# Attention and a top-1 mixture of experts on one core: the ninth block of k and q in the tile of x's transposes, and a batch's finish step by step at named places

## The chip, the core and the metric

The kernel runs on one core of a Trainium2 chip: TensorE (PE in the rows) multiplies matrices, VectorE (DVE), ScalarE (ACT) and GpSimd (POOL) work on tiles, and the queues of SyncE (SP) and GpSimd start transfers. Each engine has its own instruction stream and runs it in order; semaphores join the streams. The metric is device time in microseconds, from one execution of the whole program. Matmul results lie in PSUM; here three buffers of two banks each (`ps_s`) serve nearly all of attention.

## What is computed

Block-causal attention over 8 batches of 8 heads, 576 positions and 64 dimensions each, then a mixture of experts in which each of the 4608 rows goes to the one expert with the largest gate logit:

```python
scores = np.where(mask, scale * np.matmul(q, k.transpose(0, 1, 3, 2)), -1000000000.0)
attn = np.exp(scores - np.max(scores, axis=-1, keepdims=True))
attn = attn / (np.sum(attn, axis=-1, keepdims=True) + 1e-09)
x = np.matmul(attn, v)                      # then [B * S, H * D]

logits = x @ w_gate
e_idx = np.argmax(logits, axis=1)
probs = softmax(logits)                     # sum + 1e-9
eom = 1.0 / (1.0 + np.exp(-(x @ w_output_gate)))
for e in range(E):
    mask = e_idx == e
    h = np.maximum(x[mask] @ w1[e], 0.0)
    out[mask] = gate_w[mask, None] * eom[mask, e, None] * (h @ w2[e])
```

## The kernel before, in words

**Pairs, periods, rounds.** Attention goes over 32 pairs (8 batches by 4 pairs of heads). A pair passes through the stages fetch, turn, maxima, probabilities, values, norm, transposes of x; the pairs overlap like a pipeline. `round_of(g)` writes one round, four rounds (`r` = g mod 4) are one **period**, in which each stage handles one pair. Four periods are one **cycle**, a batch. I number periods by q = g // 4, so q mod 4 is the place in the cycle (period 0, 1, 2, 3). TensorE, ScalarE and VectorE run in the order in which the Python code is written (`manual_schedule`); GpSimd and the queues are ordered by a scheduler that follows the code.

**The period.** It begins with max_odd (L193 on TensorE, its maximum L340 on VectorE) and max_tile 0 (L186); then prob_tile 3 of the pair before (L240), norm (L293 to L297), prob_tiles 0 and 1 (L212), max_tiles 1 and 2 (L177 on VectorE) and max_rest (L198); then values_odd and values (L264 to L266). In the fourth round `turn` transposes eight of the nine 128-row blocks of a later pair's k and q into one `ps_s` tile (L123); ScalarE copies them to float16 (L127) and VectorE subtracts to get the low part (L128). `turn_max` transposes the maxima (L326) into bank 0 of another tile, puts the **ninth block** (r = 0) into bank 1 of the same tile, and converts it on VectorE (a small L127 and a small L128). `spare[0]` keeps that tile: max_odd of the next period writes its scores into both of its banks, columns 320 to 384. `turn_x` transposes a finished pair's x (L311) in a third tile, from which ScalarE copies (L313, L314). On GpSimd a period has `lpcr` and five `lpc` (L255, low parts of the probabilities, read from SBUF) and one `vl` (L151), which values need (L265). In the last four pairs the `lows` of L255 are VectorE's.

**The finish of a batch.** When a batch's x is transposed, `turn_x` hangs the generator `finish_batch` into the list `later`. Each call of `pay_later` runs one step of it, up to the next `yield`. There are eight calls in a period, three of them in the third round. The steps: gate logits `lgT` on TensorE (L494) and their copy; transposes (L502) and the sum `L` (L504); `mx` and `eq` (L510, L513); `eq` times `erev` and `er` (L515, L517); `oh` and `d` (L519 to L525); the exponential of `d` and the gate's `z` and `zs` (L527 to L531); the matmuls of the ranks (L535 to L540) and the running count (L544, L545); `rk` and `rank` (L548, L550); `sl` and `sli` (L554, L556); `se` (L560, L561); `zs` and the reciprocal (L563, L564); then five **scatters** into the slot table (`tab_d`, L567), one per step. It begins one round after the last transposes of x, which are in period 2, so nearly all of it lies in period 3.

**The seam.** The last finish runs while the first steps of the experts are being built (`ahead`), one step of each in turn. `route_rest` counts rows per expert and builds the table of steps (L584 to L720); GpSimd fetches slots (`ids`, L743) and gathers rows (`xg`, L754), which ScalarE and VectorE turn into `xr` (L866, L867) in front of `h` (L905) and `y` (L934). After that TensorE works on experts to the end.

## Time and profile before

| | |
|---|---|
| three runs, median (lowest to highest) | 817.33 us (815.25 to 818.15) |
| the profiled execution, its own time | 811.65 us |
| its span, first to last instruction | 810.0 us, granted clock 0.972 |
| busy, share of the span | PE 697.3 us (86%), DVE 558.4 (69%), ACT 444.2 (55%), POOL 405.9 (50%) |
| attention's steady cycles | from 50.78 to 320.82 us, periods 4 to 27 |
| seam between attention and experts | some 400 to 455 us |

The average of busy time hides two stages. In the second half TensorE is busy nearly throughout; in the first none of the engines is. So the rows below are taken by stage: the periods of one cycle, the waits in attention, one ordinary period and one with a finish in order of time, and a few rows of the seam. A period is cut where L340 starts on VectorE. The granted clock is 1.00 when TensorE was granted 2.4 GHz throughout a stretch; a lower share means that part of it was granted 1.2 GHz.

### The profile page before, as it was taken

What the parts mean: (1) busy time and instruction counts of PE and PEld (TensorE: products, weight loads), DVE (VectorE), ACT (ScalarE), POOL (GpSimd) and SP (SyncE); (2) the same over time, 40 slices, a digit from 0 to 9 for tenths busy, and PEclk for the clock granted to TensorE, in tenths of its full rate; (3) what the DMA queues carried; (4) which work ended last, traced back from release to release, by engine and by line L of the source; (5) the groups of instructions that cost most, each with busy time, mean ns of one, the idle gap of its engine ahead of it and who ended that gap; (6) DMA issues with size and microseconds to landing.
All of it is one profiled execution on the core that took longest, in us unless ns stands there. A gap on an engine that the chain in (4) does not pass through costs nothing. (4 is left out here: it accounts for less than half of the span.)

```text
span 810.0 us, 24437 instructions
## 1 busy us (share of the span) xinstructions
PE 697.3 (86%) x9931; PEld 517.4 (64%) x9950; DVE 558.4 (69%) x1000; ACT 444.2 (55%) x606; POOL 405.9 (50%) x404
## 2 busy tenths in 40 slices
PE   4889787879878787776796899999999999999994
PEld 3577665757667575655664566856667566686652
DVE  7577777877777877879362877956688666795530
ACT  2556454655546564545321867855587655885530
POOL 3777596987869696636725732222332343210001
PEclk9999999999999999998999999999999999999998
DMA  6555436263534635253108799789999979931601
GB/s 153 134 123 129 101 84 150 56 155 81 133 94 97 148 67 136 61 175 120 32 2 285 159 284 288 247 272 300 326 297 358 317 159 324 231 73 42 233 28 42
DMA packets 207850, 131.61 MB, mean 162 GB/s; under 512 B 161552, under 2 KB 180016, under 8 KB 207728
## 3 DMA queue, kind: packets, MB, share of 16 engines
q1 hardware_dynamic: 199680, 110.66, 49.6%
q0 software_dynamic: 8048, 19.29, 7.9%
q8 instruction: 80, 1.31, 0.8%
q14 instruction: 42, 0.34, 0.2%
HBM read 127.08 MB, written 19.34 MB: 181 GB/s over the span
## 5 line engine op out<-in xcount | busy, mean ns | idle before, releaser
L905 PEld LDWEIGHTS <-w1b 128*128 128x128 f16 (+1 forms) x2208 | 176.1, 98 | 25.1 <-DVE w1b L784 3.6
L905 PE MATMUL ps_s<-xt,w1b 128*128 128x256 f16 (+5 forms) x1920 | 175.8, 253 | 2.7 <-DVE w1b L784 2.2
L934 PE MATMUL ps_o<-w2b,hh 128*128 128x512 f16 (+1 forms) x541 | 164.9, 384 | 4.5 <-ACT hh L913 4.5
L784 DVE TENSOR_TENSOR w2b<-w2f,w2b 128x1024 bf16<-128x1024 f32 x80 | 92.6, 1219 | 88.8 <-ACT w2b L782 88.8
L255 POOL TENSOR_TENSOR lpc<-pc 128x512 f16<-128x512 f32 x140 | 140.9, 1041 | 7.6 <-ACT pc L248 7.2
L943 POOL DMA_INDIRECT out_dram<-ys,ids x38 | 49.4, 1300 | 163.0 <-ACT ys L942 89.3
L934 PE MATMUL ps_o<-w2b,hl 128*128 128x512 f16 x280 | 107.3, 383 | 1.4 <-DVE hl L914 0.5
L934 PEld LDWEIGHTS <-hh 128*128 128x128 f16 x560 | 54.9, 99 | 67.4 <-ACT hh L913 4.7
L784 DVE TENSOR_TENSOR w1b<-w1f,w1b 128x1024 bf16<-128x1024 f32 x80 | 92.9, 1216 | 3.2 <-ACT w1b L782 3.0
L177 DVE TENSOR_REDUCE nmz<-ps_s 128x2 bf16<-128x896 f32 (+3 forms) x128 | 82.7, 692 | 15.5 <-PE ps_s L193 14.9
L942 ACT ACTIVATE ys<-ps_o,ids 128x512 f32<-128x512 f32 (+1 forms) x38 | 26.1, 686 | 116.9 <-PE ps_o L934 101.5
L248 ACT ACTIVATE pc<-ps_s 128x1024 f32<-128x1024 f32 (+1 forms) x96 | 78.2, 882 | 19.5 <-PE ps_s L212 18.8
L782 ACT CAST w1b<-w1f 128x1024 f16<-128x1024 f32 x80 | 78.4, 1045 | 4.9 <-DMA w1f<-in_moe_w_dram 4.9
L128 DVE TENSOR_TENSOR tr<-ps_s,tr 128x1024 f16<-128x1024 f32 (+1 forms) x62 | 47.9, 772 | 44.2 <-ACT tr L127 43.2
L782 ACT CAST w2b<-w2f 128x1024 f16<-128x1024 f32 x80 | 77.6, 1043 | 0.1
L754 POOL DMA_INDIRECT xg<-x_d,ids x38 | 49.4, 1301 | 38.9 <-DVE xr L867 12.3
L264 PE MATMUL ps_v<-vh,pc 128*128 128x65 f16 x640 | 68.1, 198 | 0.0
L265 PE MATMUL ps_v<-vl,pc 128*128 128x64 f16 x640 | 67.7, 196 | 0.0
L266 PE MATMUL ps_v<-vh,lpc 128*128 128x65 f16 x640 | 67.4, 196 | 0.0
L255 POOL TENSOR_TENSOR lpcr<-pcr 128x640 f16<-128x640 f32 x28 | 35.2, 1257 | 62.6 <-ACT pcr L248 62.6
L264 PEld LDWEIGHTS <-pc 128*128 128x128 bf16 x640 | 60.0, 100 | 7.2 <-issue 7.1
L265 PEld LDWEIGHTS <-pc 128*128 128x128 bf16 x640 | 60.4, 101 | 0.6
(216 smaller groups left out, 1467.7 us busy)
## 6 DMA issues: line engine op xcount, KB each, us to landing
w1f<-in_moe_w_dram SPq DMA_DIRECT2D x80, 512.0 KB
w2f<-in_moe_w_dram SPq DMA_DIRECT2D x80, 512.0 KB
nat<-in_k_dram SPq DMA_DIRECT2D x64, 128.0 KB
nat<-in_q_dram SPq DMA_DIRECT2D x64, 128.0 KB
vn<-in_v_dram SPq DMA_DIRECT2D x64, 128.0 KB
x_d<-xn SPq DMA_DIRECT2D x32, 256.0 KB
vn<-in_v_dram SPq DMA_DIRECT2D x64, 32.0 KB
hh<-in_moe_w_dram SPq DMA_DIRECT2D x4, 512.0 KB
```

The source lines that it names most:

```text
L177: last_max[0] = nc.vector.tensor_reduce(o, ps[:, :, c0:c1], AX.X, ALU.max, negate=True)
L248: last_exp[0] = nc.scalar.activation(self.pt[i], ap, AF.Exp, scale=SCALE)
L255: eng.tensor_tensor(self.pl[i][:, sl], self.pt[i][:, sl], self.high(i)[:, sl], ALU.subtract)
L264: nc.tensor.matmul(o, hi, self.vh[rows, j], start=first, stop=False)
L265: nc.tensor.matmul(o[:, 0:D], hi, self.vl[rows, j], start=False, stop=False)
L266: nc.tensor.matmul(o, lo, self.vh[rows, j], start=False, stop=last)
L754: nc.gpsimd.indirect_dma_start(out=xg[i % NXG][0:width[i], h], out_offset=None, in_=x_d[0:nx, :], in_offset=IOA(ap=ids[i][0:width[i], h, 0 ...
L782: nc.scalar.copy(hi, src)
L784: eng.tensor_tensor(lo[at], src[at], hi[at], ALU.subtract)
L905: nc.tensor.matmul(ph[:, f4].rearrange("p (h n) -> p h n", n=w), wv[:, cc, f, :], xv[:, cc], start=(k == 0), stop=(k == 3 * KD - 1))
L934: nc.tensor.matmul(py, hv[:, f, h], wv[:, f, :], start=(k == 0), stop=(k == 3 * KF - 1))
L943: nc.gpsimd.indirect_dma_start(out=out, out_offset=IOA(ap=ids[i][0:w, h, 0:1].bitcast(U32), axis=0), in_=ys[0:w], in_offset=None, bounds_c ...
```

## The change

The ninth block goes from `turn_max`'s tile into that of x's transposes: `turn_rest` takes a tile, runs `turn_x`'s five transposes into it, transposes the ninth block into columns 128 to 256 of its bank 1, then lets ScalarE copy x, then converts the block on VectorE. `max_odd` still takes `turn_max`'s tile, in which only the maxima now lie. Every `yield` of `finish_batch` names a kind of place, and `pay_later(kind)` runs a step only at a place of the kind that it waits for: "m" and "n" behind max_rest, "v" behind the first values, "y" at the end of the fourth round. The running count moves ahead of the rank matmuls, the exponential of `d` behind them. Two scatters go to a step instead of one. In the loop behind the last round, `pay_later()` without a kind runs every step.

```diff
-        def turn_x(self):
+        def turn_x(self, pa):
...
-            pa = banks().rearrange("p a n -> p (a n)")
             for t in range(NT):
                 nc.tensor.transpose(pa[:, P * t:P * t + P], self.xn[:, t], ident)
+            yield
             xT = xTs[self.b]
...
     def turn_max(p):
-        z, y = pairs[p], pairs[p + 2] if p + 2 < NPR else None
+        z = pairs[p]
...
-        if y:
-            y.turn_blocks(ps[:, 1:2, 0:P], 0)
         z.qe = sb.tile([P, 640], BF16, name="qe")
         nc.scalar.copy(z.qe, pm[:, 0:640])
+
+    def turn_rest(p, p9):
+
+        ps = banks()
+        flat = ps.rearrange("p a n -> p (a n)")
+        x = pairs[p].turn_x(flat) if 0 <= p < NPR else iter(())
+        y = pairs[p9] if p9 < NPR else None
+        next(x, None)
         if y:
-            y.halves(ps[:, 1:2, 0:P], 0, nc.vector.tensor_copy)
+            y.turn_blocks(ps[:, 1:2, P:2 * P], 0)
+        next(x, None)
+        if y:
+            y.halves(ps[:, 1:2, P:2 * P], 0, nc.vector.tensor_copy)
...
-    def pay_later():
+    want = {}
+
+    def pay_later(kind=None):
         for g in list(later):
-            if next(g, later) is later:
-                later.remove(g)
+            if kind is None or want.get(g) in (None, kind):
+                want[g] = next(g, later)
+                if want[g] is later:
+                    later.remove(g)
...
     def finish_batch(b, xT):
-        yield
+        yield "v"
         lgT = sb.tile([P, S], F32, name="lgT", bufs=1)
...
         nc.scalar.copy(lgT, pm[:, 0:S])
-        yield
+        yield "y"
...
-        yield
+        yield "m"
         lg, lz = L[:, :, 0:E], L[:, :, E:2 * E]
...
         nc.vector.tensor_tensor(eq, lg, mxb, ALU.is_equal)
-        yield
...
         nc.vector.tensor_reduce(er, eq, AX.X, ALU.max)
-        yield
+        yield "n"
...
-        yield
-        nc.scalar.activation(d, d, AF.Exp)
+        yield "v"
...
-        yield
+        add = small.tile([P, E], F32, name="add")
+        nc.vector.tensor_reduce(add, oh.rearrange("p t e -> p e t"), AX.X, ALU.add)
+        nc.vector.tensor_tensor(run_cnt[:, b + 1], run_cnt[:, b], add, ALU.add)
+        yield "y"
+        nc.scalar.activation(d, d, AF.Exp)
         nc.scalar.activation(zs, zs, AF.Exp, scale=-1.0)
...
-        yield
+        yield "m"
         sl = small.tile([P, NT], F32, name="sl")
...
-        yield
+        yield "n"
         nc.vector.scalar_tensor_tensor(zs, zs, 1.0, se, ALU.add, ALU.mult)
...
             scatters.append(sc)
-            yield
+            if t % 2 == 0:
+                yield
...
         elif r == 2:
...
-            pay_later()
-            pay_later()
+            pay_later("m")
+            pay_later("n")
             do(10, "values", 0)
-            pay_later()
+            pay_later("v")
             do(6, "lows", 2)
         else:
             do(-5, "turn")
             if g < 4 * NPR:
                 turn_max(g // 4)
-            do(15, "turn_x")
-            pay_later()
+            if g < 4 * NPR + 8:
+                turn_rest(g // 4 - 3, g // 4 + 2)
+            pay_later("x")
             do(11, "values", 1)
         for fn in events.get(g, ()):
             fn()
-        pay_later()
+        pay_later("abwy"[r])
```

What this does to the streams, at three places. First TensorE at the end of an ordinary period, before (L326 the last transpose of the maxima, L123 the ninth block, L311 x's, L264 the values):

```order
L326 LDWEIGHTS nmz_97
L326 MATMUL ps_s<-identb,nmz_97 128x128
L123 MATMUL ps_s<-ident,nat 128x128
L311 MATMUL ps_s<-ident,xn 128x128 x5
L264 LDWEIGHTS pc_2136
```

and after (L327 and L310 are the old L326 and L311):

```order
L327 LDWEIGHTS nmz_97
L327 MATMUL ps_s<-identb,nmz_97 128x128
L310 MATMUL ps_s<-ident,xn 128x128 x5
L123 MATMUL ps_s<-ident,nat 128x128
L264 LDWEIGHTS pc_2103
```

The ninth block changed places with x's transposes, and tiles with them.

Second, VectorE. Before, in period 3, from the last maxima (L198) to the big conversion and what follows:

```order
L198 TENSOR_REDUCE nmz_97<-nm_2957 128x2
L515 TENSOR_TENSOR eq<-eq,erev 128x40
L517 TENSOR_REDUCE er<-eq 128x5
L519 MEMSET er 64x1
L521 TENSOR_TENSOR oh<-er,erev 128x40
L525 TENSOR_TENSOR d<-L,mx 128x40
L529 TENSOR_TENSOR z<-L,oh 128x40
L531 TENSOR_REDUCE zs<-z 128x5
L544 TENSOR_REDUCE add<-oh 128x8
L545 TENSOR_TENSOR run_cnt<-run_cnt,add 128x8
L128 TENSOR_TENSOR tr_3198<-ps_s,tr_3197 128x1024
L127 CAST tr_3197<-ps_s 128x128
```

After, the same batch one period later, in period 0 (L524 to L546 are the old L510 to L545):

```order
L198 TENSOR_REDUCE nmz_96<-nm_3237 128x2
L524 TENSOR_REDUCE mx<-L 128x5
L527 TENSOR_TENSOR eq<-L,mx 128x40
L528 TENSOR_TENSOR eq<-eq,erev 128x40
L530 TENSOR_REDUCE er<-eq 128x5
L532 MEMSET er 64x1
L534 TENSOR_TENSOR oh<-er,erev 128x40
L538 TENSOR_TENSOR d<-L,mx 128x40
L541 TENSOR_TENSOR z<-L,oh 128x40
L543 TENSOR_REDUCE zs<-z 128x5
L545 TENSOR_REDUCE add<-oh 128x8
L546 TENSOR_TENSOR run_cnt<-run_cnt,add 128x8
```

The block stands whole between the last maxima and the big conversion (L128 is the next row), where `mx` and `eq` stood earlier before. `sl` to the reciprocal stand at the same place of period 1, `L` (L518) ahead of the first maximum of period 0.

Third, GpSimd around the scatters. Before, in period 0:

```order
L255 TENSOR_TENSOR lpc_2141<-pc_2137 128x512
L567 DMA tab_d<-idg,sli 37120x2 x3
L151 TENSOR_TENSOR vl_104<-vn_99,vh_102 128x640
L567 DMA tab_d<-idg,sli 37120x2 x2
L255 TENSOR_TENSOR lpcr<-pcr 128x640
```

After, in period 1:

```order
L255 TENSOR_TENSOR lpc_2408<-pc_2404 128x512
L151 TENSOR_TENSOR vl_103<-vn_100,vh_101 128x640
L576 DMA tab_d<-idg,sli 37120x2 x5
L255 TENSOR_TENSOR lpcr<-pcr 128x640
```

All five scatters now stand behind `vl`, one period later.

## Rows read from the trace of the kernel before

**Rows 1.** Busy time by windows: the four periods of one cycle (12 to 15).

```profile
139.95:149.41 9.46, 8.55 (x205) 7.00 (x203) 8.22 (x19) 5.96 (x9) 7.29 (x7) 1.00 0.38 92
149.41:159.23 9.82, 8.54 (x205) 7.05 (x203) 7.18 (x15) 5.96 (x9) 8.88 (x9) 1.00 0.15 29
159.23:169.81 10.58, 9.65 (x221) 7.46 (x219) 7.18 (x15) 6.07 (x10) 10.58 (x11) 1.00 0.55 129
169.81:184.41 14.60, 9.63 (x216) 7.90 (x214) 11.18 (x32) 6.93 (x12) 8.75 (x8) 1.00 0.70 169
```

Columns: stretch and length in us; busy us (and instructions) of PE, PE's weight loads, DVE, ACT, POOL; granted clock; DMA share; GB/s.

**Rows 2.** The same view, whole cycles: the first, the fourth, the last.

```profile
50.78:95.19 44.41, 37.11 (x829) 30.39 (x827) 32.72 (x77) 24.96 (x39) 30.70 (x29) 0.96 0.52 123
184.41:231.93 47.52, 39.14 (x829) 31.31 (x827) 33.81 (x81) 24.93 (x39) 35.53 (x33) 0.93 0.46 107
276.38:320.82 44.44, 36.36 (x829) 29.40 (x827) 33.77 (x81) 24.93 (x39) 35.49 (x33) 1.00 0.46 106
```

**Rows 3.** TensorE's waits, 20 to 390 us: total, times, longest.

```profile
PE ps_s L535 <- DVE oh L521: 22.6, 7, 5.7
PE ps_s L193 <- DVE tr L128: 17.6, 16, 2.2
PE ps_s L311 <- DVE tr L128: 11.1, 6, 2.0
PE ps_v L265 <- POOL vl L151: 2.5, 9, 0.4
```

**Rows 4.** VectorE in time, period 13: start, length, instruction, idle before it.

```profile
155.48 0.17 DVE L198 TENSOR_REDUCE nmz<-nm 128x2 bf16<-128x4 f32 x1
157.18 1.23 DVE L128 TENSOR_TENSOR tr<-ps_s,tr 128x1024 f16<-128x1024 f32 x1 [1.54 <-ACT tr L127]
...
158.64 0.29 DVE L128 TENSOR_TENSOR tr<-ps_s,tr 128x128 f16<-128x128 f32 x1
```

**Rows 5.** TensorE in time, the end of period 13.

```profile
158.99 0.20 PE L193 MATMUL ps_s<-tr 64*128 64x64 f16 x2 [1.03 <-DVE tr L128]
```

**Rows 6.** VectorE in time, a finish (period 15), and one row of the seam.

```profile
174.98 0.19 DVE L510 TENSOR_REDUCE mx<-L 128x5 f32<-128x40 f32 x1
175.20 0.70 DVE L513 TENSOR_TENSOR eq<-L,mx 128x40 f32<-128x40 f32 x1
...
177.15 0.75 DVE L515 TENSOR_TENSOR eq<-eq,erev 128x40 f32<-128x40 f32 x1
...
178.93 0.20 DVE L529 TENSOR_TENSOR z<-L,oh 128x40 f32<-128x40 f32 x1
...
179.53 0.17 DVE L545 TENSOR_TENSOR run_cnt<-run_cnt,add 128x8 f16<-128x8 f16 x1
...
183.38 0.17 DVE L554 SCALAR_TENSOR_TENSOR sl<-er,rank 128x5 f32<-128x5 f32 x1
...
188.67 0.89 DVE L563 SCALAR_TENSOR_TENSOR zs<-zs,se 128x5 f32<-128x5 f32 x1
...
406.48 0.19 DVE L515 TENSOR_TENSOR eq<-eq,erev 128x40 f32<-128x40 f32 x1
```

**Rows 7.** GpSimd in time, from a scatter's period to the next finish.

```profile
141.75 1.25 POOL L255 TENSOR_TENSOR lpcr<-pcr 128x640 f16<-128x640 f32 x1 [4.82 <-ACT pcr L248]
143.05 5.04 POOL L255 TENSOR_TENSOR lpc<-pc 128x512 f16<-128x512 f32 x5
...
161.91 1.39 POOL L151 TENSOR_TENSOR vl<-vn,vh 128x640 f16<-128x640 f32 x1
...
173.81 5.03 POOL L255 TENSOR_TENSOR lpc<-pc 128x512 f16<-128x512 f32 x5 [0.75 <-ACT pc L248]
```

**Rows 8.** The seam in time: VectorE, GpSimd, TensorE.

```profile
431.31 0.43 DVE L715 TENSOR_REDUCE rt<-pc 128x35 f32<-128x280 f32 x1
440.36 1.08 POOL L754 DMA_INDIRECT xg<-x_d,ids  x1 [2.82 <-DMA ids<-tab_d]
446.81 0.43 PE L934 MATMUL ps_o<-w2b,hh 128*128 128x512 f16 x1 [4.54 <-ACT hh L913]
```

More of the change, by code (lines that the diff above doesn't have):

```diff
@@ L542, in finish_batch @@
         )
-        add = small.tile([P, E], F32, name="add")
-        nc.vector.tensor_reduce(add, oh.rearrange("p t e -> p e t"), AX.X, ALU.add)
-        nc.vector.tensor_tensor(run_cnt[:, b + 1], run_cnt[:, b], add, ALU.add)
-        yield
         rk = small.tile([P, NT, E], F32, name="rk")
@@ L561, in finish_batch @@
         nc.vector.tensor_scalar(se, se, 1e-9, None, ALU.add)
-        yield
+        yield "n"
         nc.vector.scalar_tensor_tensor(zs, zs, 1.0, se, ALU.add, ALU.mult)
@@ L576, in finish_batch @@
             scatters.append(sc)
-            yield
+            if t % 2 == 0:
+                yield
     def counts(col, name):
@@ L1040, in round_of @@
             if g == 4 * NPR + 9:
-                do(13, "turn_x")
+                turn_rest(NPR - 1, NPR)
         elif r == 2:
```

## The prediction, made before the changed kernel ran

> **What bounds the kernel now.** I read the busy time by windows first, since attention and experts have different limits. The four periods of one cycle of attention (one batch) last 9.46, 9.82, 10.58 and 14.60 us, 44.46 in all, and no engine fills them: TensorE is busy 36.37 us, GpSimd 35.50, VectorE 33.76 [rows 1]. The fourth period, in which almost all of a batch's finish lies, has hardly more TensorE work than the third (9.63 against 9.65) and takes 4.02 us longer: there VectorE and the waits rule. Such a cycle repeats: the first and the last of the six whole ones last 44.41 and 44.44 us, and one is 47.52 us at a granted clock of 0.93 [rows 2], so the level of 1.2 GHz was granted in a part of it. Then I asked who waits for whom on TensorE in attention [rows 3]. Two waits lead: the rank matmuls (L535) for `oh`, 22.6 us in 7, and the maxima of a new period (L193) for VectorE's L128, 17.6 us in 16; then the transposes of x (L311) for the same L128, 11.1 in 6. The change aims at all three. The wait for `vl` from GpSimd (L265) is small today, 2.5 us in 9, but it says that GpSimd is just in time.
>
> Behind about 455 us the experts begin in earnest; what is gained before that point moves their start and, as long as their weights have been loaded, the end.
>
> **The ninth block.** Today it sits in bank 1 of the tile that the next max_odd writes. In the period from 149.41 VectorE converts the eight blocks at 157.18 for 1.23 us and the ninth at 158.64 to 158.93 [rows 4]; TensorE's L193 starts at 158.99 after 1.03 us of waiting for that [rows 5]. After the change L193 needs only ScalarE's copy of the turned maxima, and max_tile 0 behind it needs the eight-block conversion, which ended at 158.41: 0.5 us earlier. What is late next is max_rest's prob_tile 3, which takes the buffer of x's transposes and so waits for the ninth block's conversion and two copies; it stands some 0.4 us behind. So I give back 0.15 to 0.2: **0.35 us per period**, bounds 0 (prob_tile 3 comes exactly as late as now) and 0.6. The ninth block turns after x's transposes instead of before; that is one matmul of the same kind at another place, so nothing. This alone is some 1.4 us a cycle, and a quiet period becomes 9.46 − 0.35 = 9.1.
>
> **The finish, period by period** (S is a period's start, cover is the time that VectorE has free). Free time lies between the last maxima and the big conversion: L198 ends at 155.65, L128 starts at 157.18, 1.5 us [rows 4].
>
> Period 3 of the cycle (the old place): it loses all but the gate logits and their sum. The logits cost TensorE 1.1 us (9.65 against 8.54 busy in rows 1) and move here, ahead of the turn; their copy goes ahead of ScalarE's conversion, 0.25 us more, and the sum L over 320 columns stands behind the small conversion and ahead of the next maxima, 0.7 with its own wait. 9.1 + 1.1 + 0.25 + 0.7 = 11.2, before GpSimd is asked.
>
> Period 0 takes `mx` to `run_cnt`. These eleven operations took 0.9 us from 174.98 to the end of `eq`, and 2.55 from 177.15 to the end of `run_cnt` at 179.70 [rows 6]: 3.4 us in 1.5 of cover, so the big conversion, and with it max_tile 0, comes 1.9 to 2.0 us later. The rank matmuls then follow, no longer waiting for `oh`, and `rk` and `rank` stand ahead of the next maxima: 0.6. 9.1 + 2.0 + 0.6 = 11.7.
>
> Period 1 takes `sl` to the reciprocal: `zs` 0.89, `sl` 0.17 and four like `run_cnt`'s 0.17 and `z`'s 0.20 [rows 6], with their gaps 2.15 us in 1.5 of cover: 9.1 + 0.7 = 9.8. Period 2 has lost the logits: 9.1.
>
> One thing can make these dearer. `eq` and L515 took 0.70 and 0.75 us while GpSimd worked on `lpc` (173.81 to 178.84 in rows 7); L515 took 0.19 at 406.48, and `z` took 0.20 at 178.93, just behind that work [rows 6]. In the new places `d`, `z`, `run_cnt` and `sl` can meet GpSimd's `lpc` or `vl`, 0.5 us each: 0 to 1.5 us in period 0, 0 to 0.5 in period 1. In period 0 `lpc` ended 8.1 us behind S (148.09 against 139.95), and in the new order `vl`, 1.39 us long, follows it at once, where `oh`, `d` and `z` stand. I take half of the upper end, 0.7: period 0 becomes 12.4. In period 1 I take 0, since what follows hides it. The Trainium skill says of this (SBUF — State Buffer, Who interferes with whom) that a VectorE instruction with both inputs in SBUF contends with a GpSimd instruction that reads SBUF. The 0.75 against 0.19 us agree, and by that rule whatever of the finish falls beside `vl` costs its upper end, 44.3 us a cycle instead of the 43.5 below.
>
> **GpSimd.** Its five scatters move one period on, and all of them behind `vl`. From the `lpcr` at 141.75 to the end of the `vl` two periods on at 163.30 they and two periods' `lpcr`, `lpc` and `vl` (7.7 us each) fill 21.55 us, so a scatter costs 1.2 and there is hardly a pause [rows 7]. That `vl` ended 4.1 us behind the start of its period (159.23) and TensorE waited at most 0.4 for one [rows 3], so I put the need at 3.9. With the scatters in period 1, where `lpcr` can start 2.25 us behind S (1.8 in the row, and the later prob_tile 3 ahead of it), that chain ends at 23.8; the values of period 3 need it at 9.8 + 9.1 + 3.9 = 22.8. TensorE waits 1.0 us: period 3 becomes 12.2. The sum is 12.4 + 9.8 + 9.1 + 12.2 = **43.5 us against 44.46**. The wait also caps it: whatever is saved in periods 1 and 2 is only waited for in 3.
>
> **The whole.** Six whole cycles lie between 50.78 and 320.82, 270.0 us. At 43.5 they would be 261.0, −9.0, of which 3 us is the one disturbed cycle; I keep half of that, for a stretch of the lower clock that can come again elsewhere, and take −7.5. The first four periods have only the ninth block: −1. The last four pairs add VectorE's own `lows` work and are bound by VectorE, which keeps its operations: −1.5 (0 to −3). At the seam to the experts [rows 8] the last finish is paid in fewer, larger steps: by its order the reciprocal and the scatters come about 1 us earlier, and the table of steps (`rt` at 431.31) no longer stands behind the second tile of x. GpSimd's second gather at 440.36 and with it `xr` and `w1b` come some 4 us earlier, and TensorE, which sat 4.54 us before 446.81, starts step 1 without that hole. Against it, ScalarE now makes four `xr` before the two `hh`. I take −3.5 of a possible 4.5, and 0 as the other bound. Together −7.5 − 1 − 1.5 − 3.5 = −13.5 from the profiled execution's 811.65. That execution is 5.7 us below the median of 817.33 and 3.6 below the fastest of the three runs; I carry the difference over to the median: 803.8, **804 us**.
>
> **Rivals.** (a) *GpSimd becomes the bound.* The scatters now all stand between `vl` and the next `lpcr`. If they start 2 us later than I think, because the reciprocal comes late, the wait for `vl` in period 3 is 3 us instead of 1 and a cycle is 45.5; six are then 273, 3 longer than now. With the seam, the end of attention and the start this is −3: 814. For it speaks that GpSimd is in time by a few tenths today; against it that GpSimd is busy only 35.50 of 44.46 us.
> (b) *Slower: VectorE's block of finish ahead of the conversion idles TensorE long enough to lose the clock.* In period 0, 3.4 to 4.9 us stand in a row ahead of the conversion that max_tile 0 needs. TensorE then idles 2 to 3.4 us at one place in every cycle. In the cycle of 47.52 us the clock was 0.93 and 3 us were lost [rows 2]. If each cycle loses half of that and a little more, 1.7 us, and the rest of the dear ends, 1.3, comes on top, a cycle is 46.5: six are 279, 9 longer than now. Less the seam's 3.5 and 1 at the start: +4.5, 822. It decides from the point at which TensorE's pause in period 0 exceeds those that pass without a lower clock today; in the fourth period of rows 1 TensorE waits for `oh` and the clock stayed at 1.00, which speaks against it.
> (c) *The finish vanishes altogether.* If the waits on VectorE are absorbed by the three buffers, a cycle goes to 9.1 four times, plus 2.05 for the logits with their copy and sum, plus half of what I add in periods 0 and 1, 40; GpSimd's floor is 35.5 and TensorE's 36.4. Six cycles then give −30, less the half stretch of lower clock −28, with the rest −34: 783.
> (d) *The change doesn't do what it says*: max_tile 0 and prob_tile 3 come as late as max_odd does now, and the finish only changes its period. Then a cycle stays at 44.5, and only the seam's gain is left, partly: 815.
>
> **How the numbers follow.** A measurement of this kernel can tell about 0.3%, 2.4 us, from no change; the three runs before lie 2.9 us apart. Chances: the forecast 0.56 (795 to 812: the rest of the dear ends and no gain at the end of attention on one side, the cheap end of period 0, the seam's 4.5 and an undisturbed clock on the other), (a) 0.16, (b) 0.12, (c) 0.09, (d) 0.07. Faster: 0.56 + 0.09 of (a), which lies on the edge, + 0.09 = 0.74; within 0.3%: 0.07 of (a) + 0.07 = 0.14; slower: 0.12. To hold 8 in 10 the range takes in the forecast, (a), (d), the mild part of (b), and a little of the way to (c): 790 to 819.
>
> **What would show it.** Right: L193's wait for L128 is gone from TensorE's list, and so is L535's for `oh`; periods of a cycle near 12.4, 9.8, 9.1, 12.2; L265's wait for `vl` grown to about 1 us per batch, only in period 3; the second gather near 436. Wrong: a granted clock below 0.97 with a drop in each period 0 points to (b); waits for `vl` of 3 us to (a); a cycle near 40 to (c); L186 or L240 waiting for L128 as long as L193 did to (d). The term that I trust least is period 0, where one row of operations decides between 11.7 and 13.2 us.

## The result and the profile after

The changed kernel takes 819.65 us (median of 20), the kernel before 812.38 (20): ratio 1.008, interval 1.0056 to 1.0103. It is slower by 0.8%, and just outside the forecast of 804 us (790 to 819). The forecast took 13.5 us off a median of 817.33, that of three runs; the twenty put the kernel before at 812.38, from which the same 13.5 would lead to 799. The profiled execution has a span of 817.7 us against 810.0 and a mean granted clock of 0.947 against 0.972.

One whole cycle in windows, in the columns of [rows 1] (periods 12 to 15 again):

```profile
135.84:147.96 12.12, 8.60 (x199) 7.21 (x200) 11.32 (x29) 6.41 (x11) 7.65 (x7) 0.97 0.53 125
147.96:160.54 12.58, 9.95 (x207) 7.84 (x206) 10.67 (x22) 5.96 (x9) 8.65 (x8) 0.90 0.41 98
160.54:172.27 11.73, 10.24 (x202) 8.10 (x199) 7.11 (x16) 6.07 (x9) 10.75 (x11) 0.85 0.48 85
172.27:183.66 11.39, 10.36 (x220) 8.13 (x221) 7.59 (x17) 6.51 (x10) 8.40 (x8) 1.00 0.51 120
```

The cycle takes 47.8 us where it took 44.46. Period 3 is 3.2 us shorter; period 0 is 2.7, period 1 2.8 and period 2 1.15 us longer. The clock of 0.90 and 0.85 gives a part of the reason for periods 1 and 2: TensorE was granted 1.2 GHz for a part of the time. TensorE's waits from 20 to 390 us, beside [rows 3] (L551 is the old L535; L186 is max_tile 0):

```profile
PE ps_s L551 <- DVE tr L128: 19.3, 6, 3.2
PE ps_s L186 <- DVE tr L128: 17.1, 17, 2.6
...
PE ps_v L265 <- POOL vl L151: 3.6, 1, 3.6
```

The waits that the change aimed at (L193 and L311 for L128, L535 for `oh`) are gone. Two others stand in their place: the rank matmuls, and max_tile 0 (L186), behind period 1 above all, now wait for the *big* conversion. The one wait for `vl` is in period 31. In time:

```profile
147.24 0.19 PE L551 MATMUL ps_s<-oh,below 128*128 128x40 f16 x1 [3.22 <-DVE tr L128]
...
160.15 0.34 PE L186 MATMUL ps_s<-tr 64*128 64x384 f16 x2 [2.58 <-DVE tr L128]
```

And in windows of one microsecond behind the first of them:

```profile
149.00:150.00 1.00, 1.00 (x32) 0.71 (x26) 0.96 (x4) 0.16 (x1) 0.00 (x0) 0.50 0.38 85
150.00:151.00 1.00, 1.00 (x18) 0.61 (x16) 0.97 (x4) 0.55 (x1) 0.38 (x1) 0.72 0.86 195
```

A granted clock of 0.50 is 1.2 GHz: behind the wait TensorE works without a gap, at half speed. Why the big conversion is late, on VectorE:

```profile
143.95 1.44 DVE L538 TENSOR_TENSOR d<-L,mx 128x40 f32<-128x40 f32 x1
...
155.04 0.38 DVE L565 SCALAR_TENSOR_TENSOR sl<-er,rank 128x5 f32<-128x5 f32 x1
155.46 0.97 DVE L567 TENSOR_SCALAR sli<-sl 128x5 int32<-128x5 f32 x1
...
156.56 0.87 DVE L570 TENSOR_SCALAR se<-se 128x5 f32<-128x5 f32 x1
157.53 1.25 DVE L572 SCALAR_TENSOR_TENSOR zs<-zs,se 128x5 f32<-128x5 f32 x1
...
158.92 1.18 DVE L128 TENSOR_TENSOR tr<-ps_s,tr 128x1024 f16<-128x1024 f32 x1
```

and GpSimd in the same time:

```profile
143.93 1.40 POOL L151 TENSOR_TENSOR vl<-vn,vh 128x640 f16<-128x640 f32 x1
...
152.36 5.04 POOL L255 TENSOR_TENSOR lpc<-pc 128x512 f16<-128x512 f32 x5 [0.48 <-ACT pc L248]
157.35 1.41 POOL L151 TENSOR_TENSOR vl<-vn,vh 128x640 f16<-128x640 f32 x1
```

Beside `lpc` or `vl`, `sl` took 0.38 us, `sli`, the addition to `se` and `zs`, all of five columns, 0.87 to 1.25, and `d`, forty columns, 1.44. From `sl` to the reciprocal's end at 159.0 it is 3.95 us.

### The profile page after: what moved, and what is told of

The parts are those of the page before. It is cut to its first block, busy times and chain, and to the rows that moved or that the text cites. A ratio compares the mean times of both kernels' runs of the same rounds, so it can differ in the third digit from the quotient of the medians.

```text
span 817.7 us, 24522 instructions
## 1 busy us (share of the span) xinstructions
PE 710.9 (87%) x9931; PEld 525.0 (64%) x9950; DVE 576.2 (70%) x1000; ACT 443.9 (54%) x606; POOL 402.1 (49%) x404
## 5 line engine op out<-in xcount | busy, mean ns | idle before, releaser
L255 POOL TENSOR_TENSOR lpc<-pc 128x512 f16<-128x512 f32 x140 | 140.9, 1040 | 5.9 <-ACT pc L248 5.1
L953 POOL DMA_INDIRECT out_dram<-ys,ids x38 | 47.2, 1242 | 160.0 <-ACT ys L952 81.2
L952 ACT ACTIVATE ys<-ps_o,ids 128x512 f32<-128x512 f32 (+1 forms) x38 | 26.1, 686 | 112.5 <-PE ps_o L944 92.8
L128 DVE TENSOR_TENSOR tr<-ps_s,tr 128x1024 f16<-128x1024 f32 (+1 forms) x62 | 47.6, 768 | 36.8 <-ACT tr L127 33.3
L764 POOL DMA_INDIRECT xg<-x_d,ids x38 | 50.6, 1331 | 41.2 <-DMA ids<-tab_d 12.6
L255 POOL TENSOR_TENSOR lpcr<-pcr 128x640 f16<-128x640 f32 x28 | 35.1, 1255 | 70.8 <-ACT pcr L248 70.7
L248 ACT ACTIVATE pcr<-ps_s 128x640 f32<-128x640 f32 x32 | 22.6, 705 | 84.5 <-PE ps_s L240 82.0
L264 PE MATMUL ps_v<-vh,pc 128*128 128x65 f16 x640 | 68.3, 198 | 0.0
L264 PEld LDWEIGHTS <-pc 128*128 128x128 bf16 x640 | 60.2, 100 | 7.5 <-issue 7.4
```

What stands on the lines that cost most here:

```text
L128: nc.vector.tensor_tensor(tl, ps, th, ALU.subtract)
L248: last_exp[0] = nc.scalar.activation(self.pt[i], ap, AF.Exp, scale=SCALE)
L255: eng.tensor_tensor(self.pl[i][:, sl], self.pt[i][:, sl], self.high(i)[:, sl], ALU.subtract)
L264: nc.tensor.matmul(o, hi, self.vh[rows, j], start=first, stop=False)
L764: nc.gpsimd.indirect_dma_start(out=xg[i % NXG][0:width[i], h], out_offset=None, in_=x_d[0:nx, :], in_offset=IOA(ap=ids[i][0:width[i], h, 0 ...
```

## The experiments

The kernel before took from 812 to 835 us in different sets of runs, and its clock differed. So each run is judged by its ratio to the kernel before in its own set.

**The two parts alone.** The ninth block on the old finish:

```diff
-            do(15, "turn_x")
+            if g < 4 * NPR + 8:
+                turn_rest(g // 4 - 3, g // 4 + 2)
             pay_later()
```

> The kernel before with the ninth block alone moved into the tile of x's transposes; the finish stays as it was. Theory (the ninth block helps, the places hurt): quiet periods of 9.2 us instead of 9.46 and the fourth period of a cycle some 1 us shorter than 14.6, since L193 no longer waits for the small conversion; a cycle of 43 to 44 us, in all 4 to 8 us faster than before, granted clock about 0.97. Rival (the ninth block itself hurts, because prob_tile 3 now waits for its conversion and two copies): quiet periods of 9.5 us or more, and a time within 3 us of before or slower.

Ratio 1.0114 (1.0038 to 1.019): *slower*, so the theory missed. Its quiet periods are 9.23 us as it said; but period 3 is 16.4 to 17.3, where the kernel before took 14.6 four times and 15.5 twice:

```profile
265.01:282.30 17.29, 12.45 (x218) 10.39 (x214) 11.19 (x31) 6.97 (x12) 8.67 (x8) 0.75 0.56 136
...
274.15 0.21 PE L545 MATMUL ps_s<-oh,below 128*128 128x40 f16 x1 [2.82 <-DVE oh L531]
```

The same wait in the kernel before, in its period 23, with the period's window:

```profile
261.77:276.38 14.61, 9.62 (x216) 7.90 (x214) 11.19 (x32) 6.93 (x12) 8.75 (x8) 1.00 0.68 163
...
270.92 0.19 PE L535 MATMUL ps_s<-oh,below 128*128 128x40 f16 x1 [2.83 <-DVE oh L521]
```

Waits of 2.82 and 2.83 us, the same instruction and cause: with one the clock fell, with the other not. The kernel before shows both by itself. The wait stands in six of its periods 3 (periods 7, 11, 15, 19, 23, 27), 2.82 or 2.83 us each; in periods 7 and 19 the clock fell at its end and the period took 15.50. Period 7:

```profile
79.69:95.19 15.50, 10.87 (x216) 8.99 (x214) 11.19 (x32) 6.96 (x12) 7.69 (x7) 0.89 0.48 113
...
88.83 0.21 PE L535 MATMUL ps_s<-oh,below 128*128 128x40 f16 x1 [2.83 <-DVE oh L521]
```

The length of a wait near 3 us does not settle whether it costs clock. One of the four that did not, in period 15, had been the ground of the forecast for holding rival (b) unlikely; the two that did lie in the cycles of 0.96 and 0.93 in [rows 2], of which the forecast took one for disturbed.

The new places with the ninth block in its old tile:

```diff
-            if g < 4 * NPR + 8:
-                turn_rest(g // 4 - 3, g // 4 + 2)
+            do(15, "turn_x")
             pay_later("x")
```

> The changed kernel with the ninth block put back into the tile of the turned maxima; the steps of the finish keep their new places. Theory (the places hurt): periods 0 and 1 of a cycle are as long as in the changed kernel or longer (12.3 and 12.8 us), the clock is as low as 0.94, the time is 8 to 14 us above that of the kernel before, so above the changed kernel too. Rival (the two parts hurt only together, because max_tile 0 now waits for the big conversion): a time at or below that of before.

Ratio 1.0165 (1.010 to 1.023), with periods 0 to 2 of 12.2, 13.0 and 10.9 us: the places hurt by themselves, as the theory said. Whether the ninth block takes some of it back is not shown: the changed kernel had 1.008 in one set of runs and 1.0139 in another.

**Clock or wait?** TensorE is given work in the two waits:

```diff
             do(11, "values", 1)
+            if 8 <= g // 4 < 28 and g // 4 % 4 < 2:
+                for j in range((28, 22)[g // 4 % 4]):
+                    nc.tensor.matmul(spare[0][:, 1, 0:256], identb, kext.rearrange("p n x -> p (n x)")[:, 0:256], start=True, stop=True)
```

> The changed kernel with matmuls added whose results nobody reads: in periods 0 and 1 of each cycle from period 8 to 27, behind the last values of the period, 28 and 22 matmuls of 256 columns into the free bank of the turned maxima's tile, so that TensorE works where it waited 3.2 and 2.6 us for VectorE. Theory (the lower clock behind these waits is what makes the periods long): the granted clock of these periods stays at 1.00, period 1 falls from 12.6 to about 11 and period 2 from 10.8 to 9.3, 2.5 to 3.5 us a cycle, so 12 to 16 us faster than the changed kernel. Rival (the waits themselves cost, the clock does not matter): periods 0 to 2 as long as in the changed kernel or longer, the time the same or 2 to 5 us more.

Ratio 0.9944 (0.9904 to 0.9984), with 50 more matmuls a cycle, some 11 us below the changed kernel's 1.008 (12 to 16 were expected). Its first cycle with them:

```profile
87.85:99.98 12.13, 11.60 (x227) 9.85 (x228) 11.34 (x30) 6.41 (x11) 7.65 (x7) 1.00 0.49 117
99.98:111.37 11.39, 11.16 (x229) 9.24 (x226) 10.67 (x23) 5.96 (x9) 8.70 (x8) 1.00 0.44 103
111.37:120.67 9.30, 8.60 (x202) 7.12 (x199) 7.11 (x17) 5.96 (x9) 8.27 (x9) 1.00 0.51 105
120.67:132.06 11.39, 10.36 (x220) 8.13 (x221) 7.59 (x18) 6.51 (x10) 10.82 (x10) 1.00 0.40 93
```

At a clock of 1.00 the changed schedule's cycle is 44.2 us: period 1 lost 1.2 and period 2 some 2.4, period 0, which the drop comes after, nothing. So about 3.6 us of the 47.8 are clock. In the four later cycles period 2 took 13.0 (at a clock of 0.87), 10.7, 10.2 and 9.2.

**VectorE's block out of the way.** `sl` to the reciprocal behind the conversion:

```diff
-        yield "m"
+        yield "y"
         sl = small.tile([P, NT], F32, name="sl")
...
-        yield "n"
         nc.vector.scalar_tensor_tensor(zs, zs, 1.0, se, ALU.add, ALU.mult)
```

> The changed kernel with the block from sl to the reciprocal moved from ahead of the big conversion of period 1 to the end of that period, behind the small conversion, where GpSimd has nothing to read. Theory (six operations took 3.95 us ahead of the conversion, stretched by GpSimd, and idle TensorE): behind it they take 1.1 to 1.5 us, the wait of 2.6 us ahead of max_tile 0 of period 2 is gone, the clock of period 2 stays at 1.00, period 2 is 9.3 us plus at most 0.7, period 1 is 1 to 2.5 us shorter; 8 to 14 us faster than the changed kernel in all. Rival (VectorE is simply late in period 1, wherever the six stand): the first maximum of period 2 comes later by what they take, and a cycle is as long as now within 1 us.

Ratio 1.0006 (0.9973 to 1.0038), by the ratios some 6 us below the changed kernel, where 8 to 14 were expected. The six took 1.3 us instead of 3.95:

```profile
157.50 0.36 DVE L565 SCALAR_TENSOR_TENSOR sl<-er,rank 128x5 f32<-128x5 f32 x1
157.90 0.17 DVE L567 TENSOR_SCALAR sli<-sl 128x5 int32<-128x5 f32 x1
...
158.41 0.17 DVE L571 SCALAR_TENSOR_TENSOR zs<-zs,se 128x5 f32<-128x5 f32 x1
```

The wait of 2.6 us is gone and period 2 is 8.6 to 9.3 us. Now something like rival (a) shows itself: the scatters come in period 2, later than in the changed kernel, TensorE waits up to 1.8 us for `vl` (7.6 us in 5), and period 3 is 12.5 to 14.8.

**The finish spread over four periods**, first with the last three batches paid at every place (`at_place` gives the kind for the batches before 5 and None for these):

```diff
         nc.vector.tensor_reduce(er, eq, AX.X, ALU.max)
-        yield "n"
+        yield at_place("y")
...
         nc.vector.tensor_tensor(d, lg, mxb, ALU.subtract)
-        yield "v"
...
-        yield "m"
+        yield at_place("y")
         sl = small.tile([P, NT], F32, name="sl")
...
-        yield "n"
         nc.vector.scalar_tensor_tensor(zs, zs, 1.0, se, ALU.add, ALU.mult)
```

> The changed kernel with the finish spread over four periods: ahead of the big conversion of period 0 only mx to er, behind it oh to the running count, behind that of period 1 the rank matmuls with rk and rank, behind that of period 2 sl to the reciprocal, the scatters in period 3; the last three batches pay a step at every place as before the change. Theory (a long block ahead of the big conversion, stretched by GpSimd, idles TensorE and loses the clock): no wait of TensorE over 1.5 us from period 7 to 27, granted clock 1.00 there, periods of about 10, 9.7, 9.7 and 11.4, a cycle of 40 to 42 us, 15 to 25 us faster than before. Rival (VectorE and GpSimd are late wherever the finish stands): cycles of 44 us or more, or a wait for vl over 1.5 us, and a time within 5 us of before.

Ratio 0.9853 (0.9785 to 0.992), faster than before, by 12.8 us and not the 15 to 25 expected. Periods 0 to 2 are 10.3, 9.0 and 10.5 at a clock of 1.00, as expected (one period 0 took 11.5); period 3 is 14 to 17, which was not, and period 27, where the first of the late batches is paid, takes 26.1. Beside it, the ninth block alone with TensorE kept busy ahead of the rank matmuls:

```diff
         pr = bank()
+        if 1 <= b < 6:
+            for j in range(24):
+                nc.tensor.matmul(pr[:, 256:512], identb, kext.rearrange("p n x -> p (n x)")[:, 0:256], start=True, stop=True)
```

> The kernel with the ninth block alone moved, and for batches 1 to 5 24 matmuls of 256 columns, whose results nobody reads, ahead of the rank matmuls, where TensorE waited 2.8 us for oh. Theory (this kernel is slow only because the clock falls in period 3 behind that wait, as it did not in the kernel before): the clock of period 3 is 1.00, period 3 takes 14.2 to 14.6 instead of 17.3, a cycle 43 to 44 instead of 47.7, 13 to 18 us faster than the ninth block alone and 4 to 10 faster than before. Rival (period 3 is long for another reason, a buffer or ScalarE): 16 us or more at a clock of 1.00.

Ratio 1.0009 (0.9973 to 1.0045). Period 3 is 15.7 at a clock of 1.00 (periods 19 and 23), between theory and rival: 1.6 us of the 17.3 were clock. The other 1.1 above 14.6 lie behind x's transposes, 3.0 us from their start to the next period where the kernel before took 1.9 (periods 19 and 23): the small conversion now waits for ScalarE's copy of x, and `rk` and `rank` stand behind it.

```profile
241.43 0.29 DVE L127 CAST tr<-ps_s 128x128 f16<-128x128 f32 x1 [1.70 <-ACT xT L314]
```

That is the rival's cause, ScalarE. Four periods 0 and 1 between 8 and 17 lost clock instead, down to 0.80.

**The end of attention.** Batches 5 to 7 paid at every place, in the changed kernel, run in two sets, the second beside the changed kernel itself:

```diff
+        def at_place(kind):
+            return kind if b < 5 else None
...
-        yield "v"
+        yield at_place("v")
```

> The changed kernel in which the batches 5 to 7 pay a step of their finish at every place, as before the change; the others keep the named places. Theory (the finish of batch 5 comes late, so the ids, the gathers, vl and GpSimd's low parts of w1 fall beside VectorE's lows, and the four lpc take 13 us): the four lpc of period 31 take 3 to 4 us again, the last norm comes 5 to 8 us earlier, 5 to 9 us faster than the changed kernel. Rival (the end of attention is longer because VectorE arrives late, whatever the finish does): the end of attention is as long as in the changed kernel within 2 us.

> The changed kernel once more, so that the runs beside it can be compared with it on the same chip. Theory: the same ratio to before as found, about 1.008; periods 0 and 1 of 12.1 and 12.6 us, four lpc of 13 us at the end of attention. Rival (the ratio depends on the chip, since the clock of the kernel before does): a ratio between 0.98 and 1.0 where before runs at a clock of 0.95.

> The changed kernel with the batches 5 to 7 paid at every place, again, beside the changed kernel. Theory: from period 24 to the last norm 5 to 8 us shorter than in the changed kernel, four lpc of period 31 in 3 to 4 us; up to period 24 the same. Rival: those periods are longer, since the steps of batch 5 then stand in periods with VectorE's lows, and the time is that of the changed kernel or more.

Ratios 1.0166 (1.0083 to 1.0248), then 1.0259 (1.0162 to 1.0356) beside 1.0139 (1.007 to 1.0207) of the changed kernel: the theory fell, paying the late batches early costs about another 1%. Periods 26 to 28 show where: 47.9 us in e10, 38.1 in the changed kernel beside it. The spread finish says the same:

> The finish spread over four periods as in e5_spread, again, beside the changed kernel. Theory: cycles of 40 to 42 us at a clock of 1.00 where TensorE has no pauses of 1 to 2 us that the profile puts to no releaser; 15 to 25 us faster than before and 20 or more faster than the changed kernel. Rival (period 3 loses the clock in any case): period 3 of 14 us or more, a cycle of 44 or more.

> The same spread finish, but the last three batches keep the named places too. Theory (a late finish of batches 5 and 6 harms the end of attention): the same cycles up to period 24 as with the late batches anywhere, then the end of attention 4 to 10 us longer, with lpc on VectorE stretched beside GpSimd's low parts of w1. Rival (the place of the last finishes does not matter): the two within 3 us.

With the late batches at every place 0.9831 (0.974 to 0.9921), with all at named places **0.9691** (0.962 to 0.9761); period 27 takes 23.3 us in the one trace and 15.1 in the other.

The changed kernel's second trace differs from its first at two places. Its periods 2, where the scatters stand, take 14.5 to 15.9 us instead of 9.2 to 11.7. And four `lpc` of period 31, which had taken 13.03 us on VectorE, took 3.91:

```profile
397.53 3.91 DVE L255 TENSOR_TENSOR lpc<-pc 128x512 f16<-128x512 f32 x4
```

From the start of period 31 to the last norm it is 38.85 us there, 44.29 in the first trace.

**TensorE's pauses.** What makes period 3 of the spread finish long (in that of e9 from 162.37, TensorE and GpSimd):

```profile
162.37:178.61 16.24, 12.65 (x188) 9.35 (x188) 7.58 (x18) 6.72 (x10) 12.57 (x12) 0.79 0.39 89
```

```profile
166.20 0.28 PE L212 MATMUL ps_s<-tr 64*128 64x256 f16 x2 [1.33 <-issue]
...
168.59 0.21 PE L264 MATMUL ps_v<-vh,pcr 64*128 64x65 f16 x1 [1.15 <-issue]
```

```profile
162.74 0.98 POOL L574 DMA_INDIRECT tab_d<-idg,sli  x1 [1.23 <-DVE nm L350]
164.02 0.97 POOL L574 DMA_INDIRECT tab_d<-idg,sli  x1 [0.30 <-issue]
...
169.00 1.00 POOL L574 DMA_INDIRECT tab_d<-idg,sli  x1 [0.17 <-issue]
```

TensorE pauses for nothing that the profile names, just behind the scatters; up to period 30 all such pauses over 0.6 us stand there, in the periods 3, and in four of the five the clock falls (0.79 here). The first trace of before has none. So before again, and the scatters one a period:

```diff
             scatters.append(sc)
+            if b < 4 and t:
+                tc.add_manual_dep(sc, last_exp[0].ins.name, SYNC, reason="one scatter a period")
-            if t % 2 == 0:
+            if b < 4:
+                yield "y"
+            elif t % 2 == 0:
                 yield
```

> The kernel before once more, with a trace of its own beside the runs of this set, since its time and its clock were 812 us in one set of runs and 833 in another. Theory (TensorE pauses behind the scatters, which the profile puts to no releaser, come with the place of the scatters): no such pauses here, or few, and cycles of 44.5 with drops of the clock in some of them. Rival (the pauses come with the set of runs, whatever the kernel): pauses of 1 us and more behind the scatters here too.

> The finish spread over four periods for all batches, as in e9_spread_all_batches, with the scatters of the batches 0 to 3 apart, one a period: each of the last four may start only behind the last exponential of its period. Theory (five scatters in a row make TensorE pause 1 to 3 us behind them, and the clock falls): the pauses are gone up to period 27, period 3 falls from 14 to 16 us to 11 to 12 at a clock of 1.00, a cycle takes 40 to 42 us, 10 to 18 us faster than the spread finish. Rival (the pauses come from the loads that are issued behind vl, not from the scatters): pauses and period 3 as they were.

> The changed kernel with the scatters of the batches 0 to 3 apart, one a period. Theory: without pauses behind the scatters period 2 is 9.2 to 11 us instead of 14.5 to 16, where only the drop behind the wait of period 1 is left; a cycle 45 to 47 us, 15 to 25 us faster than the changed kernel in its second set of runs, about the time of before. Rival (period 2 is long because of the two waits for VectorE alone): a cycle of 50 us or more.

> The changed kernel with the matmuls of e3_busy_waits, whose results nobody reads, in TensorE's two long waits, and with the scatters of the batches 0 to 3 apart. Theory (waits for VectorE and pauses behind the scatters are all that costs clock): a clock of 1.00 in all periods from 8 to 23, periods of 12.1, 11.4, 9.3 and 11.4, a cycle of 44.2, 10 to 20 us faster than before where that loses clock. Rival: drops stay, and a cycle is over 45.

Before again gave 1.0018 (0.9982 to 1.0054). In this trace there are pauses of 1.0 to 1.3 us behind its scatters in two of the periods 1, of 0.5 in the others: the pauses come with the set of runs *and* stand behind bunched scatters. Its periods 3, which hold no scatter, took 15.5 to 16.8 at 0.75 to 0.89, each with the old wait of 2.8 us for `oh`. Apart, the pauses shrink: in e11 to 0.4 us up to batch 4, whose five are still in a row and give pauses of 1.2 to 1.3 and a period of 17.4. Its period 3, scatters apart:

```profile
116.90:128.23 11.33, 9.68 (x188) 7.57 (x188) 7.46 (x17) 6.39 (x10) 9.77 (x9) 1.00 0.47 109
```

e11's ratio is 0.970 (0.9604 to 0.9796), no better than the 0.9691 of e9, where 10 to 18 us were expected: the scatter now stood ahead of `vl` and pushed it beside `oh`, behind which L350 and TensorE wait:

```profile
137.51 1.48 DVE L534 TENSOR_TENSOR oh<-er,erev 128x40 f16<-128x40 f32 x1
```

```profile
136.52 0.98 POOL L574 DMA_INDIRECT tab_d<-idg,sli  x1 [0.15 <-issue]
137.53 1.40 POOL L151 TENSOR_TENSOR vl<-vn,vh 128x640 f16<-128x640 f32 x1
```

```profile
140.78 0.50 PE L212 MATMUL ps_s<-tr 64*128 64x384 f16 x2 [2.42 <-DVE nm L350]
```

e12, the changed kernel with its scatters apart, gave 0.9939 (0.990 to 0.9979) where the changed kernel gave 1.0139 in another set; its periods 2 are 9.4 to 10.3 for the batches 0 to 3, as expected, and 15.1 for batch 4, whose scatters are in a row. e13, with both remedies, had a clock of 1.00 in every period from 8 to 23 and 0.9887 (0.9793 to 0.9981): 44.8 us in its first cycle, 45 to 48 in the others, longer than expected since a scatter ahead of `vl` lengthens period 0 there too (`run_cnt` took 1.94 us beside that `vl`).

**The version that beats both.** The scatters behind their period's `vl`, and what the ninth block is worth there:

```diff
+                tc.add_manual_dep(sc, last_vl[0].ins.name, SYNC, reason="behind the vl of the period")
...
+            elif b == 4 and t % 2:
+                yield "y"
```

> The finish spread over four periods as in e9, the scatters of the batches 0 to 4 apart, each of the later ones behind its period's vl instead of ahead of it, the fifth batch's in twos. Theory (two things were left in e11: a scatter ahead of vl pushed vl beside oh, which took 1.48 us, and batch 4's five scatters in a row): oh and run_cnt take 0.2 us each again, periods 10.3, 9.0, 10.5 and 11.4, a cycle of 41 to 42 us at a clock of 1.00 from 8 to 27, 12 to 25 us faster than e11 was against its before; ratio to before 0.945 to 0.965. Rival (GpSimd is late with one scatter a period): waits for vl or lpcr, a cycle of 43 or more, a ratio of 0.97 or above.

> The same kernel with the ninth block back in the tile of the turned maxima: what the first part of the change is worth where the finish does no harm. Theory: quiet periods of 9.46 instead of 9.24, and in period 0 to 2 L193 waits for the small conversion, with oh and sl behind it no later than now: 0.2 to 0.4 us a period, 6 to 12 us slower than with the ninth block in x's tile. Rival (the ninth block's place is worth nothing where VectorE has room): within 3 us.

e14: 783.24 us against 819.07, ratio **0.9574** (0.9527 to 0.9622). One of its cycles:

```profile
214.69:225.13 10.44, 9.32 (x231) 7.85 (x231) 9.71 (x27) 5.96 (x9) 8.09 (x8) 1.00 0.55 117
225.13:234.12 8.99, 7.85 (x167) 6.65 (x168) 7.28 (x18) 6.18 (x11) 8.12 (x8) 1.00 0.64 132
234.12:244.59 10.47, 9.56 (x239) 8.00 (x237) 8.28 (x23) 5.96 (x9) 9.23 (x10) 1.00 0.53 126
244.59:255.36 10.77, 9.67 (x188) 7.57 (x188) 7.47 (x18) 6.50 (x10) 9.95 (x10) 1.00 0.44 96
```

40.67 us; the five whole cycles from period 8 on are 40.5 to 43.6, all at 1.00. (The execution that was traced took 794.93 us; only its periods are read here.) e15, with the ninth block in its old tile, is 0.9683 (0.9616 to 0.975), 791.21 us: the ninth block's new place is worth some 8 us here, in the 6 to 12 that were expected. Not all of it need be the wait: e15 lost clock in two of its periods from 8 to 27 (0.84 and 0.87), e14 in none.

## Why the prediction was wrong, step by step

*The ninth block.* The mechanism held: L193 no longer waits for L128, and a quiet period fell from 9.46 to 9.23. The term was 0.35; it measured 0.23, within its bounds. In a quiet period max_tile 0 and prob_tile 3 now wait 0.37 and 0.26 us for L128, where L193 had waited 1.03. In period 3 of the old finish the new place costs 1.1 us (e7), a term that the sum did not need, since that finish moved too.

*Period 0, 12.4.* It measured 12.12. The half of the dear end was right in kind: `d` met `vl` and took 1.44 us. The page on SBUF of the Trainium skill that I weighed there (SBUF — State Buffer, Who interferes with whom) was borne out, also where it names copies and `tensor_scalar` as able to contend: `sli` and the addition to `se` took 0.97 and 0.87 us beside GpSimd's reads, 0.17 behind them. Left out of the sum, and given to rival (b): the pause that this leaves on TensorE, 3.2 us, costs the *next* period clock.

*Period 1, 9.8.* **The term that failed.** It took 12.6. The six operations were priced at 2.15 us from rows where GpSimd happened to be idle for most of them; their dear end was put at 0.5, for `sl` alone, and taken at nothing since "what follows hides it". They took 3.95, stretched by `lpc` and `vl`; that alone makes 11.4 (e3), and the lower clock makes the rest. Nothing hid it: the cover was to be the wait for `vl` in period 3, and that wait does not exist.

*Period 3, 12.2, and GpSimd.* It measured 11.39. The wait of 1.0 us for `vl` didn't come, because periods 1 and 2 were longer than forecast. GpSimd's chain was sized well, 21.55 us in the forecast and 22.4 from the `lpcr` at 150.62 to the end of the second `vl` behind it. Whether it would have held TensorE up by 1.0 us behind short periods no run shows; in e4, where the scatters came later still, it did by up to 1.8.

*The clock.* Rival (b) was what happened, with a chance of 0.12. It said 46.5 us a cycle and 822 us; the five cycles from period 8 to 27 took 45.4 to 47.8, and the kernel 819.65. It was held down by one observation, that a wait of 2.8 us passed at a clock of 1.00 in period 15 of the kernel before; **this was the second step that failed**, since the same wait lost the clock in periods 7 and 19 of the same trace, and in e1 each time. It was also priced as one drop a cycle, and three of the five cycles had two. That its 822 comes so near the kernel's time is luck in part: it had the six cycles at +9 and nothing at the end of attention, which measured +3.5 and +8.0. Rival (d) was not what happened: its sign, L186 or L240 waiting as long as L193 did, is missing in the quiet periods.

*The sum.* From trace to trace: the first four periods −1.2 (forecast −1); the cycle from period 4, in which the first finish now only begins, −5.3; the five behind it +8.8 (the six together +3.5, forecast −7.5); from the start of period 28 to the end of the last norm +8.0 (forecast −1.5); from there to the second gather −4.0 (forecast −3.5); the rest +1.5. Of one cycle, 47.8 against the forecast 43.5: the lower clock 3.6, period 1's stretched operations 1.6, period 2 0.2, less 0.3 in period 0 and 0.8 in period 3 (the periods at a clock of 1.00 by e3's first cycle).

*The end of attention* is **the other term that failed**, −1.5 against +8.0. Periods 28 to 30 add 0.6 of it: period 28, which carries a finish's block, is longer (12.13 against 9.73), the two behind it shorter. The other 7.4 lie between the start of period 31 and the last norm, 44.29 us against 36.91. There one of VectorE's `lpc` took 11.23 us beside GpSimd's `vl` and low parts of w1. In the second trace of the same kernel no such tile took over 1.6 us, and the stretch took 38.85. The first trace:

```profile
362.68:406.97 44.29, 26.56 (x479) 21.44 (x474) 35.49 (x62) 19.99 (x30) 31.07 (x41) 0.76 0.33 102
```

and in the second trace:

```profile
389.72:428.57 38.85, 24.63 (x479) 19.63 (x476) 30.45 (x62) 19.88 (x30) 35.08 (x41) 0.81 0.35 102
```

All seven traces of this case in which a tile of L255 on VectorE took 9 us or more there have 43.9 to 45.4 us in this stretch; of the other twelve eleven have 32.4 to 40.9, one 43.6. So some 5 of the 7.4 us go with that tile. That it is their cause no run shows, since none took it away alone, and what sends GpSimd's work beside it stays open. Paying the last finishes earlier is no remedy: it made the whole longer.

*The seam* went as forecast, counted from the last norm. The second gather:

```profile
446.62 1.08 POOL L764 DMA_INDIRECT xg<-x_d,ids  x1 [4.77 <-DMA ids<-tab_d]
```

It is 6.3 us later than in [rows 8], but the last norm was 10.3 later; TensorE's hole of 4.54 us ahead of L934 shrank to 1.0 (and its wait for the gathered rows grew from 3.6 to 5.2). It could not pay for attention.

## What to carry to other kernels

Work taken off a waiting engine's path and put ahead of a conversion that the same engine needs a moment later only moves the wait. Price each moved operation at its new place by what the neighbouring engine does *there*, and count whole pauses of TensorE: here one of 3.2 us cost another 1.2 in clock behind it and one of 2.6 another 2.4. Before a rival is held unlikely by one place in a trace, look at every place of the same kind: this wait stood six times in the trace of before, and the clock fell in two. Behind the conversion, spread over periods, and with the scatters apart, the same finish took 4% off the kernel.

## What the runs showed of the hardware that was not expected

- A wait of TensorE of 2.8 us, on the same instruction, went with a drop to 1.2 GHz in two of six periods in the first trace of the kernel before, in six of six in its second, and in six of six in e1. What decides it, these rows don't show.
- Five indirect scatters in a row were followed by pauses of TensorE that no releaser explains, 0.9 to 1.5 us in e9, and by none in the first trace of before; one a period, up to batch 4, by 0.4 (e11). Each of e11 to e14 also has one or two of 0.9 to 1.8 us, 4 to 8 us behind a scatter. The Trainium skill (Runtime: NRT & Kernel Launch, Instruction fetch mechanics) says that each engine's sequencer fetches its instructions through a DMA queue of its own; that the scatters delay this fetch is a guess, and no run here shows it.
- VectorE can be kept out for long: four `lpc` that take 2.50 us together at 388.85, with GpSimd idle for most of it, took 13.03 one group earlier, 11.23 of it one tile, while GpSimd ran from 368.92 to 379.20 without a pause. Seven traces of this case have such a tile, of 9.0 to 11.2 us:

```profile
367.33 13.03 DVE L255 TENSOR_TENSOR lpc<-pc 128x512 f16<-128x512 f32 x4
...
388.85 2.50 DVE L255 TENSOR_TENSOR lpc<-pc 128x512 f16<-128x512 f32 x4 [0.30 <-ACT pc L248]
```

```profile
368.92 1.41 POOL L151 TENSOR_TENSOR vl<-vn,vh 128x640 f16<-128x640 f32 x1
370.29 2.54 POOL L794 TENSOR_TENSOR w1b<-hh,w1b 128x256 bf16<-128x256 f32 x4
...
375.31 2.54 POOL L794 TENSOR_TENSOR w1b<-hh,w1b 128x256 bf16<-128x256 f32 x4
377.81 1.39 POOL L151 TENSOR_TENSOR vl<-vn,vh 128x640 f16<-128x640 f32 x1
```
